# Constant multiplications on TensorE ahead of the first turned rows, a later weight split and a later second search

## The chip, the cores and the metric

The kernel runs on one core of one Trainium2 chip. The metric is the device time of one execution in microseconds (us), of which the median of several runs counts. TensorE (PE) multiplies, VectorE (DVE) and ScalarE (ACT) do element-wise work and empty PSUM, GpSimd (POOL) and SyncE (SP) mostly issue transfers. Weight loads of TensorE have a row of their own, PEld.

## The reference

A spectral filter along the sequence is followed by a mixture of eight experts, in which each expert takes exactly 2496 of the 19968 tokens, in the order of all logits.

```python
X = np.fft.rfft(x, axis=1)                      # x: 8 x 2496 x 256
y = np.fft.irfft(X * F[None], n=x.shape[1], axis=1)
logits = y.reshape(N, D) @ w_gate               # N = 19968, D = 256, 8 experts
order = np.argsort(-logits.flatten())
...                                             # greedy: token and expert both still free
for e in range(E):
    mask = assigned == e
    h = np.maximum(x[mask] @ w1[e], 0.0)        # 256 x 1024
    out[mask] = h @ w2[e]                       # 1024 x 256
```

## The kernel before

The program has two parts that meet in the middle. The first part is the transform. It multiplies by the filter and transforms back in two steps. The last step (`inv2_parts`, line 375) multiplies a constant matrix `cD` of 120x120 with tiles `z` in plain f32, two 256-column groups at a time, into PSUM tiles named `pv`; ScalarE copies them to `xo` (line 376) and a transfer stores them to `xs` in DRAM.

The second part is the experts, one after the other. GpSimd gathers the expert's tokens from `xs` (`xg`, line 788), 128 rows each. `turn` transposes them on TensorE into PSUM (`ptr`, line 802), ScalarE casts the result to a high part `xo` (line 805) and VectorE subtracts it for the low part `z` (line 806). The first matrix product (`pz`, line 824) uses six passes of 512 columns for each of eight groups of 128 hidden units: weights are split in a high and a low part too (`split`: high part on ScalarE in line 781, low part on VectorE in line 782; `w0` is the first matrix, `w1` the second). ScalarE applies relu (line 830), VectorE makes the low part of the hidden values (`hl`, line 832). The second product is line 867 (`py`).

Which tokens an expert gets is found by a search (`Route.phase`): VectorE first computes, over all 117x176x8 logits, a maximum `M` (line 615), two products `tmp` (lines 617 and 619), a table `Gm` (line 530) and `ar`, `A` (lines 621 to 625); then come eleven rounds in which TensorE counts (lines 538 and 551) and VectorE narrows a threshold. `places` turns the result into row numbers in five parts, each with two pairs of small TensorE products (line 735). The first search runs beside the last inverse step; the search for the second expert is opened while the first expert starts.

Three things set the order. TensorE's order is the order in which the code is written (`manual_schedule`). What of the search is written where follows from `Pump`: each stage yields a name and a number, and the next stage is written once that much TensorE time has been counted (`'d', 5.5` is 5.5 us). The order on VectorE and ScalarE is laid down by a scheduler at build time and is fixed when the program runs: an instruction that waits holds all behind it on its engine. The list `split` holds the eight parts of an expert's weights, numbers 0 to 3 the first matrix, 4 to 7 the second. Hidden groups 0 to 3 need parts 0 and 1 alone, groups 4 to 7 need parts 2 and 3. In the expert loop one part is split every five steps (`PACE`), and `flush(8)` splits what is left before the second product.

The PSUM tiles `pv`, `ptr` and `pz` share four buffers in turn: a new one can be written when the tile four before it has been read by ScalarE and VectorE.

Of the kernel before, what the change touches and what calls it, by code (L numbers as in the profile page):

```python
# [7 lines left out]
F32, F32R = mybir.dt.float32, mybir.dt.float32r  # L8
# [432 lines left out]
class Route:  # L441
# [166 lines left out]
    def phase(s, ph):  # L608

        nc = s.nc  # L610
        v = lambda n, sh, dt=F32, bufs=2: s.wb.tile(sh, dt, name=n, bufs=bufs)

        if 0 < ph < 7:
            with s.tc.issue_after(s.last):
                nc.vector.tensor_reduce(s.M, s.lg, axis=AX.X, op=OP.max)
            yield 'd', 5.5
            nc.vector.tensor_tensor(s.tmp, s.lg, s.M.unsqueeze(2).to_broadcast([117, S, 8]), op=OP.is_equal)
            yield 'd', 1.5
            nc.vector.tensor_tensor(s.tmp, s.tmp, s.val[:117].unsqueeze(1).to_broadcast([117, S, 8]), op=OP.mult)
            yield 'd', 1.5  # L620
            nc.vector.tensor_reduce(s.ar, s.tmp, axis=AX.X, op=OP.max)
            nc.vector.scalar_tensor_tensor(s.ar, s.asg, 0.0, s.ar, op0=OP.is_equal, op1=OP.mult)
            yield 'd', 1.8
            n = s.n = 8 - ph
            nc.vector.tensor_tensor(s.A[:, :S*n].rearrange("p (s e) -> p s e", e=n), s.ar.unsqueeze(2).to_broadcast([117, S, n]),
                                    s.desc[:117, :n].unsqueeze(1).to_broadcast([117, S, n]), op=OP.is_equal)
            s.room()
            yield 'd', 1.5
# [11 lines left out]
        if ph < 7:  # L640
# [3 lines left out]
            w, P, c, q, r1 = v("w", [128, 8]), v("P", [128, 16 * n]), v("c", [128, 2 * n]), v("q", [128, 8]), v("r1", [128, 10])  # L644
# [244 lines left out]
def emit(tc, i, out):  # L889
    nc = tc.nc  # L890
    with ExitStack() as st:
# [6 lines left out]
        cD = pp.tile([120, 120], F32, name="cD")  # L898
        nc.scalar.dma_start(cD, i['cD'])
        ps = pool(st, "ps", space=PSUM)  # L900
# [41 lines left out]
        split = []  # L942
# [15 lines left out]
        with tc.manual_schedule(engines={mybir.EngineType.PE}):  # L958
            while (0, 0) not in pump.tags:
                pump.feed(0.1)  # L960
                c = next(units, None)
                pump.feed(c if c else 0.8)
            for c in units:
                pass

        with tc.issue_after(nc.gpsimd.tensor_copy(R.sidx[96:97, 19:], f.xo[96:97, 0, :1]).ins):
            W.load(0)
# [2 lines left out]
        def gather(e, g):  # L970
            pump.until((e, g))
            W.gather(e, g, pump.out[e])
        while len(split) > 4:
            W.split(*split.pop(0))
        gather(0, 0)
        with tc.issue_after(W.lastg):
# [1 line left out]
        for h in range(2):  # L978
            R.last = W.turn(0, 0, h)
        with tc.issue_after(R.last):  # L980
            while split:
                W.split(*split.pop(0))
        n = 0
        def flush(p):
# [109 lines left out]
```

## Time and profile before

| | us |
|---|---|
| median of 3 runs | 1464.4 |
| lowest and highest | 1460.85, 1466.78 |
| the profiled execution | 1464.14 |
| its span | 1461.9 |
| TensorE busy | 1387.9 |
| last inverse step ends on TensorE | 447.08 |
| first turned rows on TensorE | 458.14 |
| first product of the second matrix | 479.79 |

Times in the trace count from the start of the span. The profiled execution took 2.2 us more than its span. A plain f32 matrix product leaves two records in the trace, one for each half of its work, and the products of the experts, whose operands are stored rounded, leave one; so "x6" in a row of line 375 is three instructions. A duration includes the time in which the result drains; in a dense stream the distance from start to start is the cost.

### The profile page before, as it was taken

How to read it: one execution, taken by the hardware profiler on the slowest of the kernel's cores; microseconds unless marked ns; L12 is line 12 of the kernel's file. 1: busy time of each engine (PE TensorE's matmuls, PEld its weight loads, DVE VectorE, ACT ScalarE, POOL GpSimd, SP SyncE). 2: the span in 40 equal slices, each digit the busy share in tenths (PEclk: the TensorE clock that was granted, in tenths of full speed). 3: DMA queues.
4: the chain of work that ended last, by engine and by line, in shares of the span. 5: the costliest groups of instructions: out<-in, count | busy, mean ns of one | idle time of the engine just before them, and what ended most of it. 6: DMA issues, size and time to landing. Idle time of an engine off the chain costs nothing.

```text
span 1461.9 us, 27147 instructions
## 1 busy us (share of the span) xinstructions
PE 1387.9 (95%) x10310; PEld 1214.2 (83%) x10310; DVE 912.8 (62%) x2589; ACT 682.9 (47%) x1676; POOL 493.2 (34%) x530
## 2 busy tenths in 40 slices
PE   4999999998896999999999999999999999999998
PEld 4998899985543898888889888898888899989988
DVE  3665666753666768767876977967876845333231
ACT  3666666644565425434533633633632635433232
POOL 0343333440102413522632443443325433333212
PEclk9999999998997999999999999999999999999999
DMA  9665564559996102212211211211211321111100
GB/s 266 182 165 141 145 176 99 119 157 280 297 352 219 57 26 91 64 36 75 69 43 58 73 50 48 86 48 41 98 34 54 132 70 46 39 48 49 42 23 27
DMA packets 56248, 150.60 MB, mean 103 GB/s; under 512 B 10824, under 2 KB 31432, under 8 KB 51921
## 3 DMA queue, kind: packets, MB, share of 16 engines
q0 software_dynamic: 17840, 60.34, 12.7%
q10 hardware_dynamic: 29407, 46.10, 10.5%
q1 hardware_dynamic: 8872, 42.44, 10.3%
q8 instruction: 81, 1.33, 0.4%
q14 instruction: 48, 0.39, 0.1%
HBM read 85.17 MB, written 63.70 MB: 102 GB/s over the span
## 4 chain that ended last, share of the span: by engine, by line
PE 68%; DVE 9%; issue 9%; ACT 6%; DMA 4%; ACTq 2%; POOL 2%; POOLq 0%; SPq 0%; DVEq 0%
PE py L867 23%; PE pz L824 22%; PE p L201 4%; PE pv L375 4%; PE p L214 4%; PE pa L269 2%; ACT Y L207 2%; PE rt L538 2%; PE ptr L802 2%; ACTq L283 2%; PE pa L233 2%; POOL out L878 1%; DMA xs<-xo 1%; ACT lg L698 1%; DMA wr<-w,widx 1%
## 5 line engine op out<-in xcount | busy, mean ns | idle before, releaser
L867 PE MATMUL py<-w1h,hl 128*128 128x256 f32 x2496 | 482.6, 286 | 1.1 <-DVE hl L835 1.0
L867 PEld LDWEIGHTS py<-w1h,hl 128*128 128x128 f32 x2496 | 401.1, 191 | 3.9 <-DVE hl L835 1.7
L867 PE MATMUL py<-w1l,hl 128*128 128x256 f32 (+1 forms) x1280 | 359.1, 282 | 0.0
L878 POOL DMA_INDIRECT out<-y,oid x160 | 171.9, 1074 | 495.6 <-ACT y L877 461.2
L830 ACT ACTIVATE hl<-pz 128x512 fp32r<-128x512 f32 (+1 forms) x320 | 187.2, 587 | 229.7 <-PE pz L824 206.1
L824 PE MATMUL pz<-xo,w0h 128*128 128x512 f32 (+1 forms) x640 | 263.9, 412 | 6.5 <-DVE hl L832 4.8
L832 DVE SCALAR_TENSOR_TENSOR hl<-pz,hl 128x512 fp32r<-128x512 f32 x256 | 174.9, 687 | 127.4 <-ACT hl L830 126.5
L824 PE MATMUL pz<-xo,w0l 128*128 128x512 f32 (+1 forms) x640 | 248.5, 388 | 0.0
L824 PE MATMUL pz<-z,w0h 128*128 128x512 f32 (+1 forms) x640 | 248.2, 388 | 0.3 <-DVE z L806 0.3
L867 PEld LDWEIGHTS py<-w1l,hl 128*128 128x128 f32 (+1 forms) x1280 | 241.1, 188 | 1.9
L788 POOL DMA_INDIRECT xg<-xs,xid x160 | 176.4, 1102 | 127.0 <-issue 44.5
L877 ACT COPY y<-py 128x256 f32<-128x256 f32 x152 | 56.4, 372 | 302.2 <-PE py L867 278.9
L207 ACT COPY Y<-p 64x240 f32<-64x240 f32 (+1 forms) x304 | 116.0, 382 | 60.7 <-PE pv L242 15.7
L824 PEld LDWEIGHTS pz<-xo,w0h 128*128 128x128 f32 x640 | 121.6, 190 | 24.8 <-DVE hl L832 6.2
L824 PEld LDWEIGHTS pz<-xo,w0l 128*128 128x128 f32 x640 | 120.6, 188 | 23.7
L824 PEld LDWEIGHTS pz<-z,w0h 128*128 128x128 f32 x640 | 121.7, 190 | 16.2 <-DVE z L806 0.9
L201 PE MATMUL p<-cS,xr 117*128 117x120 f32 x688 | 103.0, 299 | 29.3 <-ACT Y L207 20.1
L201 PEld LDWEIGHTS p<-cS,xr 117*128 117x128 f32 x688 | 93.7, 212 | 33.7 <-ACT Y L207 22.8
L222 POOL TENSOR_TENSOR P<-P 128x256 f32<-128x256 f32 x80 | 58.5, 732 | 172.4 <-DVE P L220 171.3
L530 DVE TENSOR_TENSOR Gm<-M,thr 117x1232 bf16<-117x1232 f32 (+2 forms) x80 | 104.4, 1315 | 0.2
L214 PE MATMUL p<-cW,Y 128*128 128x128 f32 x640 | 89.1, 278 | 0.7 <-ACT Y L207 0.7
L214 PEld LDWEIGHTS p<-cW,Y 128*128 128x128 f32 x640 | 80.2, 193 | 2.3 <-issue 1.0
(216 smaller groups left out, 2008.6 us busy)
## 6 DMA issues: line engine op xcount, KB each, us to landing
zd<-zt ACTq DMA_DIRECT2D x160, 128.0 KB
z<-zd SPq DMA_DIRECT2D x26, 600.0 KB
xs<-xo ACTq DMA_DIRECT2D x22, 600.0 KB
xr<-x SPq DMA_DIRECT2D x7, 1344.0 KB
xr<-x SPq DMA_DIRECT2D x7, 1064.0 KB
xs<-Y ACTq DMA_DIRECT2D x10, 600.0 KB
F<-filt ACTq DMA_DIRECT2D x2, 1280.0 KB
xg<-xs,xid POOLq DMA_INDIRECT x160, 2.8
```

Source lines behind the costliest of these rows:

```text
L201: s.lastmm = nc.tensor.matmul(p[:, q-q0, :120], xv[:, q-24*h], s.cS1, start=True, stop=True).ins
L207: (nc.vector.tensor_copy if t in ((5,) if b else (1, 3, 5, 7, 9)) else nc.scalar.copy)(dst, src)
L214: nc.tensor.matmul(p[:, k], s.Y1[b][:, 4*g+k, dh*128:dh*128+128], s.cW[:, 4*g+k], start=True, stop=True)
L222: nc.gpsimd.tensor_tensor(P[:, :, :64], P[:, :, :64], P[:, :, 64:], op=OP.subtract)
L375: nc.tensor.matmul(p[:120, :w], s.cD, z[:, g-g0:g-g0+w], start=True, stop=True)
L530: nc.vector.tensor_tensor(Gm[:, s0:s1, :m], s.M[:, s0:s1].unsqueeze(2).to_broadcast([117, s1 - s0, m]), thr[:117].unsqueeze(1).to_broadcas ...
L788: s.lastg = s.nc.gpsimd.indirect_dma_start(out=xg[:n], out_offset=None, in_=s.xs, in_offset=bass.IndirectOffsetOnAxis(ap=ids[0][:n, t:t+1] ...
L824: nc.tensor.matmul(p[:, :n], w[:, sl], x[:, k, :n], start=m == 0, stop=m == 5)
L830: s.lasta = nc.scalar.activation(h[:, :n], p[:, :n], AF.Relu).ins
L832: nc.vector.scalar_tensor_tensor(l[:, :n], p[:, :n], 0.0, h[:, :n].bitcast(F32), op0=OP.max, op1=OP.subtract)
L867: nc.tensor.matmul(p[:a.stop-a.start], hs[g][f][:, a], b[:, 256*f:256*f+256], start=m == 0, stop=m == 8 * len(terms) - 1, skip_group_check ...
L878: st = nc.gpsimd.indirect_dma_start(out=out_rows, out_offset=bass.IndirectOffsetOnAxis(ap=ids[1][:w, 4*g+t:4*g+t+1], axis=0), in_=y[:w], i ...
```

## The change

Behind the last inverse step, 26 products of the constant `cD` with itself (read four times side by side, 480 columns) are written to TensorE; nothing reads their result, which takes one turn of the four shared PSUM buffers. Of the first expert's first matrix only parts 0 and 1 are split ahead of the first gather, parts 2 and 3 now behind the first turned rows, and the four parts of the second matrix are left to the expert loop. The stage of the second search that computes `M` is written 5.0 us of counted TensorE time later.

```diff
@@ phase(s, ph)
         if 0 < ph < 7:
+            if ph == 1:
+                yield 'd', 5.0
             with s.tc.issue_after(s.last):
                 nc.vector.tensor_reduce(s.M, s.lg, axis=AX.X, op=OP.max)
             yield 'd', 5.5
@@ emit
             for c in units:
                 pass
+            p = ps.tile([128, 4, 120], F32, name="pv", tag="c", bufs=4)
+            for _ in range(26):
+                nc.tensor.matmul(p[:120], cD, cD.unsqueeze(1).to_broadcast([120, 4, 120]), start=True, stop=True)
...
-        while len(split) > 4:
+        while len(split) > 6:
             W.split(*split.pop(0))
         gather(0, 0)
...
         with tc.issue_after(R.last):
-            while split:
+            while len(split) > 4:
                 W.split(*split.pop(0))
```

In the changed program the lines behind the first insertion have numbers higher by 2, so line 782 reads 784, and the constant products stand in line 969.

TensorE between the last inverse step and the first expert, before:

```order
L735 MATMUL rt<-tab_3684,OH 128x180
L375 MATMUL pv<-z,cD 120x512
L375 MATMUL pv<-z,cD 120x256
L375 MATMUL pv<-z,cD 120x512
L802 MATMUL ptr<-id,xg 128x128 x8
L824 MATMUL pz<-xo,w0h 128x512
```

and now:

```order
L737 MATMUL rt<-tab_3684,OH 128x180
L375 MATMUL pv<-z,cD 120x512
L375 MATMUL pv<-z,cD 120x256
L375 MATMUL pv<-z,cD 120x512
L969 MATMUL pv<-cD 120x480 x26
L804 MATMUL ptr<-id,xg 128x128 x8
L826 MATMUL pz<-xo,w0h 128x512
```

The 26 products stand ahead of the transposes of the first gathered rows.

VectorE from the first weight parts on, before (the low parts of weights are `w0l`, `w1l`, of turned rows `z`, of hidden values `hl`):

```order
L782 TENSOR_TENSOR w0l<-wr_5198,w0h 128x512 x4
L806 TENSOR_TENSOR z<-ptr,xo 128x2x256 x2
L615 TENSOR_REDUCE M<-lg 117x176
L617 TENSOR_TENSOR tmp<-lg,M 117x1408
L530 TENSOR_TENSOR Gm<-M,ic 117x528
L782 TENSOR_TENSOR w1l<-wr_5199,w1h 128x512 x3
L619 TENSOR_TENSOR tmp<-tmp,val 117x1408
L782 TENSOR_TENSOR w1l<-wr_5199,w1h 128x512
L832 SCALAR_TENSOR_TENSOR hl<-pz,hl 128x512 x3
L621 TENSOR_REDUCE ar<-tmp 117x176
L806 TENSOR_TENSOR z<-ptr,xo 128x2x256
```

and now:

```order
L784 TENSOR_TENSOR w0l<-wr_5198,w0h 128x512 x2
L808 TENSOR_TENSOR z<-ptr,xo 128x2x256 x2
L784 TENSOR_TENSOR w0l<-wr_5198,w0h 128x512 x2
L617 TENSOR_REDUCE M<-lg 117x176
L834 SCALAR_TENSOR_TENSOR hl<-pz,hl 128x512
L619 TENSOR_TENSOR tmp<-lg,M 117x1408
L530 TENSOR_TENSOR Gm<-M,ic 117x528
L834 SCALAR_TENSOR_TENSOR hl<-pz,hl 128x512
L784 TENSOR_TENSOR w1l<-wr_5199,w1h 128x512
L834 SCALAR_TENSOR_TENSOR hl<-pz,hl 128x512
L621 TENSOR_TENSOR tmp<-tmp,val 117x1408
L808 TENSOR_TENSOR z<-ptr,xo 128x2x256
```

Two of the four weight parts and three of the four `w1l` moved behind the first turned rows, the first hidden values moved ahead, and `M` and both `tmp` still stand behind the turned rows.

ScalarE in the same place, before:

```order
L781 CAST w0h<-wr_5198 128x512 x4
L805 CAST xo<-ptr 128x2x256 x2
L781 CAST w1h<-wr_5199 128x512 x4
L830 ACTIVATE hl<-pz 128x512 x3
L805 CAST xo<-ptr 128x2x256
```

and now:

```order
L783 CAST w0h<-wr_5198 128x512 x4
L807 CAST xo<-ptr 128x2x256 x2
L832 ACTIVATE hl<-pz 128x512 x2
L783 CAST w1h<-wr_5199 128x512
L832 ACTIVATE hl<-pz 128x512
L807 CAST xo<-ptr 128x2x256
```

The casts of the second matrix moved from ahead of the first three relus to between them.

## Rows read from the trace of the kernel before

**Rows 1.** Page, part 1: busy us (share of the span) x instructions.

```profile
PE 1387.9 (95%) x10310; PEld 1214.2 (83%) x10310; DVE 912.8 (62%) x2589; ACT 682.9 (47%) x1676; POOL 493.2 (34%) x530
```

**Rows 2.** Stretches: us, busy time by engine, granted clock, DMA share, GB/s.

```profile
447.10:458.10 11.00, 0.00 (x0) 0.00 (x0) 0.64 (x5) 1.74 (x6) 5.14 (x7) 0.59 0.80 266
458.10:470.40 12.30, 9.36 (x30) 6.69 (x30) 12.06 (x16) 6.96 (x14) 4.85 (x5) 0.68 0.42 140
470.40:480.00 9.60, 9.60 (x48) 7.55 (x49) 9.60 (x21) 5.04 (x15) 0.00 (x0) 1.00 0.01 2
...
449.00:450.00 1.00, 0.00 (x0) 0.00 (x0) 0.00 (x0) 0.00 (x0) 0.87 (x1) 0.51 0.94 312
...
466.00:467.00 1.00, 1.00 (x5) 0.76 (x4) 1.00 (x3) 1.00 (x3) 0.00 (x0) 0.96 0.00 0
```

**Rows 3.** Timeline, TensorE, 442 to 445: start, us, what [idle before].

```profile
442.41 2.34 PE L375 MATMUL pv<-z,cD 120*120 120x512 f32 x6
444.58 0.32 PE L735 MATMUL rt<-tab,OH 117*128 117x180 f16 x2
```

**Rows 4.** Timeline, TensorE, from the last inverse step to the second matrix.

```profile
444.74 2.34 PE L375 MATMUL pv<-z,cD 120*120 120x512 f32 x6
458.14 2.10 PE L802 MATMUL ptr<-id,xg 128*128 128x128 f32 x8 [11.07 <-DMA xg<-xs,xid]
460.92 0.79 PE L824 MATMUL pz<-xo,w0h 128*128 128x512 f32 x1 [0.68 <-ACT xo L805]
...
462.65 0.63 PE L824 MATMUL pz<-xo,w0l 128*128 128x512 f32 x1
463.08 0.63 PE L824 MATMUL pz<-xo,w0h 128*128 128x512 f32 x1
...
470.40 0.50 PE L824 MATMUL pz<-xo,w0h 128*128 128x512 f32 x1 [1.88 <-DVE hl L832]
...
479.79 0.28 PE L867 MATMUL py<-w1h,hl 128*128 128x256 f32 x1
```

**Rows 5.** Timeline, VectorE, from the first weight parts on.

```profile
458.30 2.50 DVE L782 TENSOR_TENSOR w0l<-wr,w0h 128x512 fp32r<-128x512 f32 x4 [10.50 <-ACT w0h L781]
460.72 1.28 DVE L806 TENSOR_TENSOR z<-ptr,xo 128x512 fp32r<-128x512 f32 x2
461.92 1.61 DVE L615 TENSOR_REDUCE M<-lg 117x176 f32<-117x1408 f32 x1
463.56 1.62 DVE L617 TENSOR_TENSOR tmp<-lg,M 117x1408 f32<-117x1408 f32 x1
465.10 0.70 DVE L530 TENSOR_TENSOR Gm<-M,ic 117x528 bf16<-117x528 f32 x1
...
469.67 1.88 DVE L832 SCALAR_TENSOR_TENSOR hl<-pz,hl 128x512 fp32r<-128x512 f32 x3
471.46 1.61 DVE L621 TENSOR_REDUCE ar<-tmp 117x176 f32<-117x1408 f32 x1
```

**Rows 6.** Two pieces of the chain that ended last, and ScalarE's first casts.

```profile
473.82 0.44 PE ptr L802 x4
474.26 4.79 PE pz L824 x21
...
459.74 1.12 ACT L805 CAST xo<-ptr 128x512 fp32r<-128x512 f32 x2
```

**Rows 7.** Second expert: a gather, its landing (588 to 594), the transposes.

```profile
589.78 0.96 POOL L788 DMA_INDIRECT xg<-xs,xid  x1 [0.30 <-issue]
...
xg<-xs,xid POOLq DMA_INDIRECT x4, 3.2
...
599.62 0.60 PE L802 MATMUL ptr<-id,xg 128*128 128x128 f32 x4
```

**Rows 8.** Waits of TensorE, 500 to 1462: total us, times, longest.

```profile
PE pz L824 <- DVE hl L832: 2.9, 2, 1.5
...
PE rt L538 <- DVE Gm L530: 0.2, 1, 0.2
```

## The prediction

> **What bounds the kernel now.** I read the page's busy times first, then stretches around the change, then the timelines of TensorE, VectorE and ScalarE there. TensorE is busy 1387.9 of 1461.9 us [rows 1], so only a place where it stands still, or runs slowly, can give much. The change is at such a place. TensorE does nothing from 447.1 to 458.1 [rows 2]: it has to wait for the first gathered rows [rows 4]. The granted clock drops to 0.51, the lower of its two levels (1.2 of 2.4 GHz), and is back only in the stretch from 466 [rows 2]. Passes of 512 columns meanwhile follow each other at 0.43 us (462.65 to 463.08) [rows 4], against 4.79 / 21 = 0.228 us later [rows 6]. A second loss follows at 470.40, where TensorE waits 1.88 us for VectorE's `hl` [rows 4], because VectorE is full: 12.06 of 12.30 us, then 9.60 of 9.60 [rows 2]. Transposes end, the first product needs the casts, and the second matrix starts at 479.79 [rows 4]. That start is my yardstick: behind it the orders of TensorE's own work agree but for the search.
>
> **The constant products.** Three inverse products with 512, 256 and 512 columns (six records) start at 442.41 and the next work starts at 444.58 [rows 3], 2.17 us for 1280 columns or 1.70 ns a column. The constant products are of the same kind, plain f32 with `cD` as weights, so one costs 480 x 1.70 = 0.81 us and 26 cost 21.2 us. They need nothing and start when the last inverse product has gone in, at 446.9 (its end, 447.08 [rows 4], less some 0.16 of draining). They end at 468.1. The gap they fill is only 11.07 us [rows 4]. So the first transposes go from 458.14 to 468.1: **+9.96 us**. The rows and weights wait for TensorE instead of the reverse.
>
> **What the full clock gives.** Nothing lets TensorE idle ahead of the rows, so I take the clock as full from there. Before, transposes began at 458.14 and the fourth hidden group (the one that waited for `hl`) at 470.40 [rows 4], 12.26 us. Now: two sets of four transposes at 0.44 [rows 6] end at 469.0; the two casts take 1.12 [rows 6] and end at 469.9; the two `z` (1.28 [rows 5]) end at 470.65; six passes of 0.228 each for group 0, of which the first ran before that, end at 471.85, groups 1 and 2 at 473.2 and 474.6, four more transposes at 475.05, where group 3 could begin. That is 6.95 us instead of 12.26: **-5.31 us**. It has the slow passes, the slow transposes and the wait of 1.88 in it. The later split is hidden here: parts 0 and 1 (0.62 each, 2.50 / 4 [rows 5]) are done near 459.6, and TensorE comes only at 468.1. Without the constant products the split would be worth about the 1.2 us of two parts.
>
> **What VectorE then holds up.** VectorE's order is fixed, and in it `M`, both `tmp` and `Gm` stand behind the two `z`, which now can't come before 469.35. So its 10 us of free time are lost, and its list meets the first groups again. From 470.65, by the distances in [rows 5]: two weight parts 1.24, `M` 1.64, `hl` of group 0 0.60, `tmp` 1.54, `Gm` 0.62, `hl` of group 1 0.60 (done 476.8), one `w1l` 0.62, `hl` of group 2 (478.0), second `tmp` 1.54, `z` of the next rows (480.15), `hl` of group 3 (480.85), one `w1l`, a one-hot table of 0.7 and small ones, `hl` of group 4 (482.8), `ar` 1.54, next `z` (484.95). TensorE against it, by the four shared PSUM buffers: group 3 runs 475.05 to 476.6 (with 0.17 for a `places` pair); group 4 needs the buffer that `hl` of group 1 frees at 476.8, wait 0.2; after it the transposes end at 478.8; group 5 needs the buffer of the turned rows that `z` frees at 480.15, wait 1.35; groups 6 and 7 run to 484.25; the ninth group needs the second `z` at 484.95, wait 0.75. Then 1.37 and a pair of 0.17: the second matrix starts at 486.55, 11.5 us behind group 3 instead of 9.39 (479.79 - 470.40) [rows 4]: **+2.1 us**. If the VectorE list cost nothing this term would be 0. At the other end, the last quarter of the second matrix and `hl` of group 7 come from VectorE at about 488.6 and are wanted at 488.85; a slip of 1.5 us there would add some 1.3. I take the walk. The second matrix's casts stand between the relus on ScalarE; that engine is not full and none of its entries is last in the walk.
>
> **The later second search.** It moves some 5 to 6 us of TensorE work later, in all later searches too. Searches and `places` lie beside the expert products, and I cost this at nothing, as long as the second expert's rows still come in time (third case below). TensorE's waits behind 500 add up to 11.3 us in ten rows, from 2.9 to 0.2 [rows 8]. They come of such meetings and will be dealt anew; that is worth 2 us either way. SP issues nothing new, and GpSimd's gathers and weight transfers for the first expert keep their order.
>
> **Sum.** 9.96 - 5.31 + 2.1 = +6.75. On the profiled execution's own 1464.14 us (2.2 more than its span, 0.3 below the median of the runs) that is 1470.9 us, 0.4% slower.
>
> **The rivals.** First, the constant products are short. If one cost a single record, 0.41 us, 26 would take 10.6 us and end at 457.5, just when the rows come. The whole walk would shift by 10.0 less 0.15 for the second `w0l` part that is then last, and the second matrix would start 3.1 us earlier than before: 1461.0. For it speaks how well it fits the gap; against it that the same kind of product leaves two records and costs 1.70 ns a column [rows 3]. Chance 0.06. The Trainium skill, page "TensorE: Matmul & The Clock Gate", section "Back-to-back issue gap", gives N/2.4 + 2.5 ns for an isolated product at the full clock, which for 480 columns is 0.2 us, an estimate of 5.3 us for all 26. By that they would end near 452.3, TensorE would idle again and only VectorE's new order would be left, some 1 to 2 us faster; [rows 3] show four times that price for f32, so I don't use it.
>
> Second, the other side, slower by over 0.5%: **the second expert's second rows come late**. Its last gather for the first half of those rows is issued at 589.78, lands 3.2 us later at 593.0, and is turned at 599.62 [rows 7], so 6.6 us of room. The pair of `places` products that this gather rests on stood 88 passes of the second matrix (0.118 each, half a 512-column pass), 36 of the first, eight transposes, a count and four pairs ahead of the turn, 20.1 us. Now 70, 18, eight and three pairs, 13.6 us, so 6.5 of the 6.6 are used. Each of VectorE's 1.6 us entries that slips in front takes about that much from TensorE. One or two would add 1.5 to 3: 1472.4 to 1473.9. Chance 0.17.
>
> Third, the moved searches meet VectorE better than before and give back 2 to 4.5 of those 11.3 us: 1466.4 to 1468.9. Nothing speaks for it but that some of it may. Chance 0.12. Fourth, the same and more, or the products are free, so that over 7.3 us are gained: below 1457. Chance 0.03, since the idle gap has to stay whatever TensorE does in it.
>
> **How the numbers follow.** My forecast has 0.62, with its own range from 1468.8 (VectorE's list costs nothing) to 1472.3 (the slip at 488.6). The bound of 0.5%, about what a measurement of this kernel can tell from no change, lies at 1471.7; a quarter of my own case is above it. Slower by over 0.5%: 0.155 + 0.155 of the second rival = 0.31. Faster by over 0.5%: 0.03. Within: 0.66. The range of 8 in 10 runs from 1466, the low end of the third rival, to 1475, the second rival on top of the slip. The first and the fourth are left out.
>
> **What would show it.** Right: 52 records of line 969 at about 0.41 us from 447 to 468, no drop of the granted clock, first transposes at 468, TensorE waits of 1 to 2 us on `z` or `hl` before the second matrix, which starts near 486.5. Wrong: the constant products end before 460; or the second matrix starts before 483, which would mean that VectorE's list does not matter; or TensorE waits for gathered rows near 606.

## The result and the profile after

The changed kernel took 1471.78 us in the median, against 1463.05 us for the kernel before; the ratio is 1.0053 with a 95% interval of 1.0037 to 1.0068. It is slower by about 7.8 us if the ratio is taken, 5.4 to 9.9 by its interval; the two medians lie 8.7 us apart. The prediction had 1470.9 us, 6.75 us over the profiled execution.

The profiled execution of the changed kernel took 1469.33 us, its span 1467.1. Its page, part 1 (busy us, share of the span, instructions), answers to [rows 1]:

```profile
PE 1401.6 (96%) x10362; PEld 1216.2 (83%) x10362; DVE 913.0 (62%) x2589; ACT 684.5 (47%) x1676; POOL 490.6 (33%) x530
```

TensorE is busy 13.7 us more and has 52 records more: 26 constant products with two records each. The kernel got slower with a busier TensorE, because what it is busy with is nobody's result.

TensorE's timeline from the last inverse product to the second matrix (start, us, what [idle before]) answers to [rows 4]. The last inverse product ends at 443.24 in this execution (440.90 + 2.34), and the records of line 969 follow it.

```profile
440.90 2.34 PE L375 MATMUL pv<-z,cD 120*120 120x512 f32 x6
443.07 21.09 PE L969 MATMUL pv<-cD 120*120 120x480 f32 x52
464.00 1.04 PE L804 MATMUL ptr<-id,xg 128*128 128x128 f32 x8
465.77 0.50 PE L826 MATMUL pz<-xo,w0h 128*128 128x512 f32 x1 [0.73 <-ACT xo L807]
466.60 0.50 PE L826 MATMUL pz<-z,w0h 128*128 128x512 f32 x1 [0.33 <-DVE z L808]
...
470.57 0.60 PE L804 MATMUL ptr<-id,xg 128*128 128x128 f32 x4
470.93 0.48 PE L826 MATMUL pz<-xo,w0h 128*128 128x512 f32 x1
...
476.01 0.50 PE L826 MATMUL pz<-xo,w0h 128*128 128x512 f32 x1 [1.06 <-DVE loc L738]
...
480.73 0.50 PE L826 MATMUL pz<-xo,w0h 128*128 128x512 f32 x1 [0.35 <-DVE z L808]
...
482.43 0.28 PE L869 MATMUL py<-w1h,hl 128*128 128x256 f32 x1
```

There is no wait for gathered rows any more (11.07 us in [rows 4]); the transposes start the moment the constant products are through, 20.76 us behind the last inverse product instead of 11.06. The stretches of this execution (us, busy time of TensorE, weight loads, VectorE, ScalarE, GpSimd, granted clock, DMA share, GB/s) answer to [rows 2]:

```profile
443.20:464.00 20.80, 20.80 (x53) 9.35 (x52) 1.98 (x8) 3.51 (x10) 9.86 (x11) 1.00 0.65 210
464.00:471.00 7.00, 5.94 (x32) 4.66 (x30) 5.74 (x7) 3.01 (x6) 0.00 (x0) 1.00 0.00 0
471.00:482.40 11.40, 9.99 (x48) 7.12 (x47) 11.40 (x21) 7.71 (x19) 0.00 (x0) 1.00 0.01 3
```

The clock is 1.00 in all three (0.59 and 0.68 in the first two of [rows 2]), VectorE has next to nothing to do for 20.8 us (1.98 busy), and in the third stretch it is full for 11.40 of 11.40.

From the profiles, three stretches make the difference of the spans, in us:

| | before | changed | difference |
|---|---|---|---|
| start to the end of the last inverse product | 447.08 | 443.24 | -3.8 |
| to the start of the second matrix | 32.71 | 39.19 | +6.5 |
| from there to the end | 982.1 | 984.7 | +2.6 |

The first is put down to chance: nothing in it was changed, and over the ten profiles taken on chips with like times, the two above and the eight of the experiments up to early13, it lies between 442.8 and 449.6. The second is the change. The third was taken apart below.

### The profile page after: what moved, and what is told of

Read it like the earlier page. It is cut to its first block, busy times and chain, and to the rows that moved or that the text cites. A ratio compares the mean times of both kernels' runs of the same rounds, so it can differ in the third digit from the quotient of the medians.

```text
span 1467.1 us, 27248 instructions
## 1 busy us (share of the span) xinstructions
PE 1401.6 (96%) x10362; PEld 1216.2 (83%) x10362; DVE 913.0 (62%) x2589; ACT 684.5 (47%) x1676; POOL 490.6 (33%) x530
## 3 DMA queue, kind: packets, MB, share of 16 engines
q0 software_dynamic: 17840, 60.34, 12.8%
## 4 chain that ended last, share of the span: by engine, by line
PE 71%; DVE 10%; issue 6%; ACT 6%; DMA 3%; ACTq 2%; POOL 1%; POOLq 0%; DVEq 0%; SPq 0%
PE py L869 26%; PE pz L826 24%; PE pv L375 4%; PE p L201 3%; PE p L214 3%; ACT Y L207 3%; PE rt L538 2%; PE pa L269 2%; ACTq L283 2%; PE ptr L804 2%; PE pv L969 1%; PE pa L233 1%; DMA xs<-xo 1%; POOL out L880 1%; DVE Y L207 1%
## 5 line engine op out<-in xcount | busy, mean ns | idle before, releaser
L790 POOL DMA_INDIRECT xg<-xs,xid x160 | 170.9, 1068 | 117.7 <-PE ptr L804 38.6
L201 PE MATMUL p<-cS,xr 117*128 117x120 f32 x688 | 96.8, 286 | 30.0 <-ACT Y L207 19.4
L201 PEld LDWEIGHTS p<-cS,xr 117*128 117x128 f32 x688 | 87.7, 199 | 34.2 <-ACT Y L207 22.6
```

What stands on the lines that cost most here:

```text
L201: s.lastmm = nc.tensor.matmul(p[:, q-q0, :120], xv[:, q-24*h], s.cS1, start=True, stop=True).ins
L790: s.lastg = s.nc.gpsimd.indirect_dma_start(out=xg[:n], out_offset=None, in_=s.xs, in_offset=bass.IndirectOffsetOnAxis(ap=ids[0][:n, t:t+1] ...
```

## The experiments

The theory (A) was that the constant products are themselves what comes last: the time above the kernel before is their length beyond the arrival of the rows, less what the clock gives, plus what VectorE's list then costs. The rival (B) was that the later second search costs the time and the products matter little. A rival C was that VectorE's list, not TensorE, sets the pace behind the first rows (the text for n39 calls it B). A name in brackets behind a heading is the run's. For each run the ratio is to the kernel before on the same chip, and "middle" is the stretch from the end of the last inverse product to the start of the second matrix (32.71 before, 39.19 changed); it comes from one profile of each run.

**Half the constant products (n13).**

```diff
-            for _ in range(26):
+            for _ in range(13):
```

> The changed kernel with 13 constant products instead of 26, all else as in it. Theory A (the products themselves are what comes last: 0.81 us each, and 13 of them, 10.5 us, end just when the gathered rows land): first transposes about 11 us behind the last inverse product, as before, full granted clock, and the time about 9.5 us below the changed kernel, 1461 to 1463. Rival B (the later second search costs the time, by new waits of TensorE in the experts, and the products matter little): 1468 or more, with the start of the second matrix earlier but waits behind it larger.

Measured: 1462.48 us, ratio 0.9989 [0.9972, 1.0006]; middle 30.20. The 13 products, with the later search still in, take away 9.3 us, and 9.0 of them in the middle: the rival B falls. TensorE's timeline, and stretches of one us (columns as above):

```profile
446.82 10.63 PE L969 MATMUL pv<-cD 120*120 120x480 f32 x26
457.76 1.10 PE L804 MATMUL ptr<-id,xg 128*128 128x128 f32 x6 [0.31 <-DMA xg<-xs,xid]
459.51 0.44 PE L804 MATMUL ptr<-id,xg 128*128 128x128 f32 x2 [0.64 <-DMA xg<-xs,xid]
460.63 0.49 PE L826 MATMUL pz<-xo,w0h 128*128 128x512 f32 x1 [0.67 <-ACT xo L807]
```

```profile
461.00:462.00 1.00, 0.77 (x4) 0.56 (x4) 1.00 (x3) 0.00 (x0) 0.94 (x1) 1.00 0.93 393
462.00:463.00 1.00, 1.00 (x4) 0.78 (x3) 1.00 (x2) 0.00 (x0) 0.76 (x1) 0.53 1.01 426
463.00:464.00 1.00, 1.00 (x4) 0.73 (x3) 1.00 (x2) 0.60 (x1) 0.69 (x2) 0.50 0.81 328
```

The products end just when the rows land, as meant, and the clock still falls, at 462, while TensorE is busy again; one part of the expectation (full clock) was wrong.

**Half as many again (n39).**

```diff
-            for _ in range(26):
+            for _ in range(39):
```

> The changed kernel with 39 constant products. Theory A: 13 more at 0.81 us stand in the path, so 10.5 us more than the changed kernel, about 1482, ratio to the kernel before 1.0125. Rival B: VectorE's list, not TensorE, is last behind the first rows, so a later start of the transposes is partly made up: under 1477.

Measured: 1482.20 us, ratio 1.0120 [1.0089, 1.0150]; middle 49.66, 10.47 us over the changed kernel for 13 products, 0.805 us each. The whole of it arrives at the end. TensorE, and not VectorE, sets the start of the rows, and VectorE's list makes up for none of it: the rival C falls.

**No constant product (n0).**

```diff
-            p = ps.tile([128, 4, 120], F32, name="pv", tag="c", bufs=4)
-            for _ in range(26):
-                nc.tensor.matmul(p[:120], cD, cD.unsqueeze(1).to_broadcast([120, 4, 120]), start=True, stop=True)
```

> The changed kernel without any constant product: later split and later search alone. Theory A: the granted clock falls as in the kernel before, TensorE's passes go slowly for some 7 us, the split saves about 1 us: the second matrix starts 0 to 2 us earlier than before relative to the last inverse product, and the time is 1461 to 1465. If the full clock is worth much more than the 3 to 4 us that the slow passes of before show, n0 would be clearly slower than n13, by over 5 us. Rival B: 1467 or more, since the later search is in it.

Measured: 1465.03 us, ratio 1.0008 [0.9990, 1.0027]; middle 32.39. The later split and the later search together are no gain and no loss that can be measured. With 13 products the middle is 2.2 us shorter than with none, in one profile of each. In the times the two intervals overlap.

**The second search on VectorE ahead of the turned rows, all 26 products kept (early26).** In the code, `M` is tied to `R.last`, which the turned rows overwrite; the edit leaves it at the first part of row numbers.

```diff
-            R.last = W.turn(0, 0, h)
-        with tc.issue_after(R.last):
+            turned = W.turn(0, 0, h)
+        with tc.issue_after(turned):
```

> The changed kernel, with the opening of the second search on VectorE no longer tied to the first turned rows, so that M, both tmp, Gm, ar and A run in the time in which VectorE has nothing to do. All 26 constant products stay. Theory A with the term for VectorE's list (+2.1 us in the prediction): the waits of TensorE between the fourth hidden group and the second matrix vanish, and that stretch falls from 11.5 to 9.4 us: about 1469.5, 2 us under the changed kernel. If VectorE's list does not matter, no difference.

Measured: 1467.99 us, ratio 1.0024 [1.0006, 1.0043]; middle 37.11, 2.08 us less than the changed kernel. TensorE's waits in this kernel between the first products and the second matrix (468 to 485; total us, times, longest):

```profile
PE pz L826 <- ACT xo L807: 0.7, 1, 0.7
PE pz L826 <- DVE z L808: 0.3, 1, 0.3
```

Only the two that belong to the first turn are left; the 1.06 and 0.35 of the changed kernel are gone. So the third term of the prediction was VectorE's list, and it is there because `M`, `tmp`, `Gm`, `ar` and `A` wait behind turned rows that they do not need.

**The constant products alone (c_only).**

```diff
             for c in units:
                 pass
+            p = ps.tile([128, 4, 120], F32, name="pv", tag="c", bufs=4)
+            for _ in range(26):
+                nc.tensor.matmul(p[:120], cD, cD.unsqueeze(1).to_broadcast([120, 4, 120]), start=True, stop=True)
```

> The kernel before with the 26 constant products alone: weights split as before, second search as before. Theory A: the transposes stand 20.9 us behind the last inverse product as in the changed kernel; the split of all weight parts has 10 us of free time on VectorE and ScalarE, but the scheduler puts the four parts of the second matrix behind the first turned rows, ahead of the first hl, so TensorE waits there instead. Start of the second matrix 38 to 41 us behind the last inverse product (32.7 before, 39.1 changed), 1469 to 1473. Rival B: if the later search costs most of the change, 1466 or less.

Measured: 1472.51 us, ratio 1.0046 [1.0026, 1.0066]; middle 38.49. Most of the change's cost without its other two parts. The single times spread: four of the twelve lie at 1465 to 1466, near the kernel before, the other eight at 1468 to 1476, and the profile is of one of the eight (1475.13); why is open.

**The later split alone (s_only).**

```diff
-        while len(split) > 4:
+        while len(split) > 6:
...
-            while split:
+            while len(split) > 4:
```

> The kernel before with the later weight split alone. Theory A: the turned rows come earlier by up to the 1.2 us of two weight parts, the clock is low as before, the wait for hl at the fourth group stays: 0 to 2 us faster, 1462 to 1464. If the split mattered more than that, under 1460.

Measured: 1463.39 us, ratio 0.9986 [0.9967, 1.0005]; middle 31.57, 1.1 us less than before. One step of the expectation was wrong: the wait of 1.88 us for `hl` at the fourth group did not stay. It is gone, and another came two groups later:

```profile
474.22 0.50 PE L824 MATMUL pz<-xo,w0h 128*128 128x512 f32 x1 [0.87 <-DVE loc L736]
```

From the transposes to the fourth group it is 10.55 us (12.26 before), from there to the second matrix 10.51 (9.39 before).

**The later second search alone (q_only).**

```diff
         if 0 < ph < 7:
+            if ph == 1:
+                yield 'd', 5.0
```

> The kernel before with the later opening of the second search alone. Theory A: the order on VectorE at the first rows does not change by it, so the start of the second matrix is where it was; behind it TensorE's 11 us of waits are dealt anew: within 2.5 us of the kernel before, 1461.5 to 1466.5. Rival B: 1467 or more, which would make it the main cause.

Measured: 1465.90 us, ratio 1.0016 [1.0001, 1.0032]; middle 32.57, as before. Behind the second matrix the waits are dealt anew. TensorE's waits from 500 to 650, in the kernel before:

```profile
PE rt L538 <- DVE A L625: 0.5, 1, 0.5
PE pz L824 <- DVE loc L736: 0.5, 1, 0.5
```

with the later search alone:

```profile
PE pz L826 <- DVE z L808: 2.9, 1, 2.9
PE rt L538 <- DVE Gm L530: 2.0, 2, 1.1
PE py L869 <- DVE hl L837: 0.2, 1, 0.2
```

and in the changed kernel, with the rows of VectorE and TensorE (start, us, what) that show where the longest of its waits comes from:

```profile
PE pz L826 <- DVE z L808: 2.8, 1, 2.8
PE rt L538 <- DVE Gm L530: 2.0, 2, 1.1
PE py L869 <- DVE hl L837: 0.2, 1, 0.2
```

```profile
597.11 1.60 DVE L623 TENSOR_REDUCE ar<-tmp 117x176 f32<-117x1408 f32 x1
598.64 0.67 DVE L808 TENSOR_TENSOR z<-ptr,xo 128x512 fp32r<-128x512 f32 x1
```

```profile
599.36 0.79 PE L826 MATMUL pz<-z,w0h 128*128 128x512 f32 x1 [2.80 <-DVE z L808]
```

`ar` of the third expert's search now stands just ahead of the second half of the second expert's first turned rows. The split alone keeps the two waits of 0.5. Further on less is waited: from the second matrix to the end 11.8 us in all before, 12.8 in the changed kernel, 12.9 with the search alone.

In the changed kernel this wait costs more than its 2.8 us. The granted clock falls behind it (columns as above), and the passes of 512 columns follow each other at 0.43 us until 602.5:

```profile
599.00:600.00 1.00, 0.64 (x2) 0.54 (x3) 1.00 (x7) 0.53 (x4) 0.69 (x2) 0.54 0.26 86
600.00:601.00 1.00, 1.00 (x4) 0.81 (x3) 1.00 (x7) 0.06 (x1) 0.70 (x2) 0.50 0.33 102
601.00:602.00 1.00, 1.00 (x4) 0.80 (x3) 0.97 (x3) 0.10 (x1) 1.00 (x1) 0.50 0.45 131
602.00:603.00 1.00, 1.00 (x5) 0.73 (x4) 0.50 (x2) 0.50 (x1) 0.69 (x2) 0.75 0.00 0
```

All seven profiles with the later search up to early13 have a wait of 2.8 or 2.9 us there. Behind it the clock fell in five of them (changed kernel, n13, n39, n0, early13), which take 984.7 to 986.3 us from the second matrix to the end; it stayed at 1.00 in two (early26 and the search alone), which take 983.5 us each. Without the later search, the kernel before takes 982.1 us, with its clock up from 500 to 1450; the split alone and the constant products alone take 983.4 and 984.8, with one fall of the clock each in other places (830 to 840, 690 to 700). So of the +2.6 us in the table some 1.4 go with the later search and some 1.2 with the clock, an estimate from these single profiles.

**13 products with the search early on VectorE (early13).** The edits of the first and the fourth experiment together.

> 13 constant products, and the opening of the second search on VectorE no longer tied to the first turned rows; the split and the later search as in the changed kernel. Theory A: transposes when the rows land, full clock, no waits for VectorE up to the second matrix: it starts 8 to 9 us behind what n13 has for VectorE's list less 2 us, that is some 27 us behind the last inverse product (32.7 before): 1459 to 1461, the fastest of all. If VectorE's list is not what held the groups up, no faster than n13 (1462.5).

Measured: 1464.78 us, ratio 1.0005 [0.9987, 1.0024]; middle 31.59, not 27. The expectation failed at the clock. In this execution TensorE waited 1.12, 0.50, 0.74 and 0.68 us for rows and the first cast:

```profile
446.45 10.63 PE L969 MATMUL pv<-cD 120*120 120x480 f32 x26
458.20 0.67 PE L804 MATMUL ptr<-id,xg 128*128 128x128 f32 x4 [1.12 <-DMA xg<-xs,xid]
459.37 0.41 PE L804 MATMUL ptr<-id,xg 128*128 128x128 f32 x2 [0.50 <-DMA xg<-xs,xid]
460.52 0.69 PE L804 MATMUL ptr<-id,xg 128*128 128x128 f32 x2 [0.74 <-DMA xg<-xs,xid]
461.89 0.79 PE L826 MATMUL pz<-xo,w0h 128*128 128x512 f32 x1 [0.68 <-ACT xo L807]
```

The granted clock went to 0.50 at 460 and came back only within the microsecond from 466. The rows also came later than in n13, and the early search may have to do with it. The second gather of the first expert takes 2.21 us here, while VectorE makes `A`:

```profile
453.94 1.44 DVE L627 TENSOR_TENSOR A<-ar,row 117x1232 bf16<-117x1232 f32 x1
454.00 2.21 POOL L790 DMA_INDIRECT xg<-xs,xid  x1 [0.30 <-issue]
```

In all three kernels with the search early on VectorE that gather lies beside `A` and takes 1.89 to 2.21 us (early15, early26 and this one); in the other eleven profiles it takes 0.95. Those behind it are put off by as much. With 26 products the rows are covered all the same; with 13 or 15 the wait for them grows. That `A` is what holds the gather up is read from the overlap and not tested.

The last four runs were on a chip on which the kernel before takes 1494.75 us; only their ratios compare with those of the others.

**15 products, search early on VectorE, and not later in TensorE's order (early15).**

The edits of the first experiment (with 15 in place of 13) and of the fourth together, and the two lines `if ph == 1: yield 'd', 5.0` taken out.

> 15 constant products (12.2 us, so that they end about when the second half of the gathered rows is there), the later split, the second search opened on VectorE ahead of the turned rows, and not written later in TensorE's order. Theory A: the granted clock does not fall (with 13 it fell 1 to 4 us behind the rows), TensorE's waits for VectorE up to the second matrix are gone: it starts 27 to 28.5 us behind the last inverse product (32.7 before), and behind it the waits of TensorE are those of the kernel before, 11 to 12 us: 4 to 5 us faster than the kernel before, ratio 0.997. If the clock falls here too: 31 us and ratio 1.0.

Measured: 1485.50 us, ratio 0.9930 [0.9903, 0.9957]; middle 31.18 in its profile, where the second gather took 1.89 us and the clock fell again, within the microsecond from 462, so the expected 27 to 28.5 was missed while the time is better than expected. It has the lowest ratio of all, but its middle explains only 1.3 us of the 9 between the medians (32.44 in the second profile of before); where the rest is stays open.

**15 products and the later split (n15).**

The first experiment's edit with 15, and the same two lines taken out.

> 15 constant products and the later split, the second search as in the kernel before (behind the turned rows on VectorE, not later in TensorE's order). Theory A: full clock throughout, VectorE's list still costs about 2 us between the fourth group and the second matrix: 29 to 30 us behind the last inverse product, ratio 0.998, some 2 us behind early15.

Measured: 1489.51 us, ratio 0.9961 [0.9938, 0.9984]; middle 30.45, half a microsecond above the expected range, and 2.0 less than the 32.44 of before; the rest of the 5.8 us that the ratio gives lies elsewhere, and where is open. The clock stayed at 1.00. TensorE had no wait for rows, with as many products as early15: the second gather took 0.95 us, and the fourth was issued 9.7 us behind the inverse step (11.2 in early15). The first waits are for the cast and for `z`:

```profile
448.02 12.24 PE L967 MATMUL pv<-cD 120*120 120x480 f32 x30
460.10 1.04 PE L802 MATMUL ptr<-id,xg 128*128 128x128 f32 x8
461.86 0.49 PE L824 MATMUL pz<-xo,w0h 128*128 128x512 f32 x1 [0.72 <-ACT xo L805]
462.70 0.50 PE L824 MATMUL pz<-z,w0h 128*128 128x512 f32 x1 [0.34 <-DVE z L806]
...
472.23 0.50 PE L824 MATMUL pz<-xo,w0h 128*128 128x512 f32 x1 [1.07 <-DVE loc L736]
```

The 1.07 at 472.23 is VectorE's list again.

**Both kernels once more, for second profiles.**

> The kernel before once more, for a second profile. If the rest behind the start of the second matrix (982.1 us in the first profile) is a property of the program, it comes within 0.5 us again; if it wanders by 1 to 2 us from run to run, differences of that size between kernels say nothing. The time up to the last inverse product (447.1 us) is expected to wander by some 3 us.

> The changed kernel once more, for a second profile: 39.2 us from the last inverse product to the second matrix within 0.3 us, the same waits of TensorE in the second expert (2.8 us on z). Behind the second matrix 984.7 us, within 0.5 us if this stretch belongs to the program, or 1 to 2 us away if it wanders.

Measured: middles of 32.44 and 39.20, so that stretch belongs to the program, to 0.3 us. Behind the second matrix 1011.3 and 1010.0 us, with TensorE waiting 29.9 and 28.5 us instead of 11.8 and 12.8: on this chip the long stretch is 25 to 29 us longer for both, and the order between them turns round. So the third row of the table above, +2.6 us, is not settled by single profiles. What is measured of the later search is the ratio 1.0016 of the run with it alone. By their ratios the three parts alone make +6.7, -2.1 and +2.3 us (products, split, search), 7.0 together against 7.8 for the change, each uncertain by 2 to 3 us.

## Why the prediction was right

**The constant products** were priced at 0.81 us and 21.2 us in all; they took from 443.07 to the transposes at 464.00, 20.93. Forecast for the later start of the transposes was +9.96; measured +9.70 (20.76 - 11.06). n39 shows the same price for 13 more, and that it arrives in full.

**The full clock**: forecast 6.95 us from the transposes to the fourth group instead of 12.26. Measured 6.93 (464.00 to 470.93). The clock did not fall up to the second matrix. As the prediction says, the term holds the wait of 1.88 us for `hl` too; the products alone have 7.13 (c_only), so they bring nearly all of it.

**VectorE's list**: forecast 11.5 us from the fourth group to the second matrix instead of 9.39. Measured 11.50 (470.93 to 482.43). The forecast put 0.2, 1.35 and 0.75 us there, at group 4, group 5 and the ninth group. Marked are 1.06 and 0.35 at the last two, but a marked wait begins only when the product before it has drained. From start to start, against early26, in which VectorE's list holds up nothing there, the three places cost 0.18, 1.33 and 0.62 us, so places and sizes were right to 0.13. (At 476.01 the trace names `loc`, which ended within 0.1 us of the `z` that the forecast names; n39 has `z` in that place, 1.07.) early26 took the term away and the middle went down by 2.08.

**The sum** of the three was +6.75; the middle grew by 6.48 in one pair of profiles and by 6.76 in the other.

**The later search** was costed at nothing, give or take 2 us. Alone it has a ratio of 1.0016 [1.0001, 1.0032], 2.3 us with 0.1 to 4.7 as the bounds, so the zero was too low, by about the margin that the prediction gave it. The 11.3 us of waits that [rows 8] bracket were indeed dealt anew, as the text said, and came out 1 us worse in the first profile, which speaks against the third rival too; that a new wait would also cost clock, as at 599, the prediction didn't have. It may be why the ratio gives 7.8 us and not 6.75, but the interval of the change holds both numbers, so this is not shown.

**Where luck helped.** The time of 1470.9 us came within 0.9 of the measured 1471.78, while the increase was 1.0 too small by the ratio: it was added to one execution of 1464.14, and the median of the kernel before was 1463.05. The prediction gave 0.66 to a change within 0.5% and 0.31 to one above it. The measured 0.53%, with 0.37 to 0.68 as its interval, decides nothing between the two.

**The second rival** named the second expert's second rows as the place. The gathered rows came in time, and TensorE waited 2.8 us at 599.36 for `z` of the expert's first rows, behind a 1.6 us entry of the search on VectorE. But the rival's reckoning of the room held. In the run with the search alone the gather in question, its landing in us and the turn are (GpSimd, transfer, TensorE):

```profile
593.94 0.96 POOL L790 DMA_INDIRECT xg<-xs,xid  x1 [0.30 <-issue]
xg<-xs,xid POOLq DMA_INDIRECT x4, 3.0
595.02 0.50 PE L826 MATMUL pz<-z,w0h 128*128 128x512 f32 x1 [2.91 <-DVE z L808]
599.18 0.60 PE L804 MATMUL ptr<-id,xg 128*128 128x128 f32 x4
```

The rows are there near 596.9 and are turned at 599.18. Without its wait of 2.91 us TensorE would have come to them near 596.3, an estimate from these rows. So the room of 6.6 us was used up, and the wait for `z` hid it.

The first rival (a single record for each product) is refuted by the 52 records. By the formula of the Trainium skill, page "TensorE: Matmul & The Clock Gate", section "Back-to-back issue gap", 26 products would have taken 5.3 us, an estimate; the trace has 20.93 for this plain f32 form, and the measurement decides.

## What to carry to other kernels

Filler work on an engine has to be shorter than the wait that it fills: measure the wait and the price of one piece in the same trace, count records and not instructions, and stop when the last of the awaited data lands. Here the wait was 11.07 us and the pieces 0.81; 26 of them put the rows off by 9.7 us and gave back 5.3 through the clock and the wait that went, and 13 made the middle 2.2 us shorter than none. Before filling a wait, look at what another engine leaves undone in it: VectorE was busy for 1.98 of 20.8 us, and an early start of work that was tied to the wrong event took 2 us off the path in the same place. Then look at what the moved work now meets: here a gather of the awaited rows took 0.9 to 1.3 us longer beside it.

## What the runs showed of the hardware that was not expected

The granted clock fell without a long gap. In n13 TensorE had waited 0.31, 0.64, 0.67 and 0.23 us between the end of the products at 457.45 and the dense passes from 461.69 on, and the clock went to 0.53 in the stretch from 462 and was 0.50 in the next two; in n15 waits of 0.72 and 0.34 left it at 1.00. In early15, with as many products as n15, it fell again after waits of 0.78, 0.68 and 0.22. So in these profiles the products kept the clock only where they also covered the wait for the last rows, and with 15 of them that changed with the time at which the rows came. Second, the same wait does not always cost clock: behind the 2.8 or 2.9 us in the second expert it fell in five of seven profiles and stayed at 1.00 in two. Third, a gather on GpSimd that lay beside VectorE's 1.44 us entry for `A` took 1.89 to 2.21 us in three profiles, against 0.95 in the eleven in which it did not. Fourth, the kernel before took 1464.10 and 1464.99 us in the median on two chips and 1494.75 on another. TensorE's waits behind the second matrix were 11.8 us in its first profile and 29.9 in the one from the slow chip, which makes single profiles from different chips useless for differences of a few microseconds.
